# Filler products on TensorE, first loads in another order, and the third batch's attention moved: one-core linear attention with two MoE layers

## The chip, the cores and the metric

The kernel runs on one core of a Trainium2 chip. A core has five engines that run side by side, each through its own instructions in order: PE (TensorE, matrix products; PEld is its weight load), DVE (VectorE), ACT (ScalarE), POOL (GpSimd) and SP (SyncE, which here only issues DMAs). They wait for each other through semaphores. The metric is the device time of one execution in microseconds (us), lower is better.

## The reference, cut to what matters

```python
kv  = einsum('bhsd,bhse->bhde', k, v)            # 8 batches, 8 heads, 576 tokens, 64 wide
out = einsum('bhsd,bhde->bhse', q, kv)
x   = out / sqrt(mean(out*out, -1) + 1e-6) * g_norm     # as 4608 tokens x 512
h = x @ w_in;   x = relu(h)**2 @ w_out           # layer 1: 512 -> 2048 -> 512
h = x @ w_in2;  out = (h * cos(h)) @ w_out2      # layer 2
```

q, k, v and g_norm are float32, the four weight matrices float64.

## The kernel before, in words

**Numbers.** A float64 weight is turned into two float32r halves, high and low (`words`, `value`, the end of `conv_steps`: lines L111 to L125 and L205/L206, on DVE and ACT). Activations are split likewise, so that a product is three PE products: high by high, high by low, low by high. The attention of the first two batches is done in plain float32 (L288, L314), which PE runs as several passes; later batches split the squares too (L292, L316, L317).

**Stages.** First come attention and the first two 512-token tiles of layer 1, then more attention between the tiles of layer 1, and last a recursive block scheme for the rest of both layers, which the change doesn't touch. In layer 1 a *chunk* is one 128-wide slice of the 2048 hidden units for one tile, 8 chunks to a tile. Chunk n has an in part (12 products, L379, into a PSUM bank `l` or `acc`), then relu and square on ACT (L388, L390), the split into `gh` (ACT, L393) and `gl` (DVE, L394), and, two chunks later, an out part (12 products, L416, into `acc`).

**Attention.** For one batch, 5 pieces of k and v (`kvld`) are loaded and multiplied into a 128x128 block per head pair (`kv_mm`, L258), which ACT copies to `kvx` (L271). Then 8 units follow, (p, half) with p = 0..3 a pair of heads: the product with q (`att_a`, L288), square and scaled copy on ACT (`sq` L299, `og` L300), the sum over a head by a product with a matrix of ones (`att_b`, `ss`, L314), the inverse root on ACT (`r` L319, its square L321), three DVE steps (`att_c`, L329 to L331, the last writes `xo`), the split into `xh` (ACT, L348) and `xl` (DVE, L349), and a DMA of `xo` to memory by POOL (`att_e`, L355). There are three `xo` buffers, so the fourth unit writes a buffer that the first one's DMA has to have left.

**What sets the order.** A table of times, in units of chunks, holds all jobs beside the chunks (`at(n, fn, ...)`): `starts` gives for each batch the time of its first unit and the step to the next, a weight's conversion stands at `w_at`, the load of a tile of x at `load_x`. The tile framework then makes of this an order for every engine, with its own list of what is ready. It doesn't change at run time.

**Loads.** SP issues nearly all loads, in order. It keeps eight DMAs in flight: each issue waits for the landing of the one eight before it, and for its buffer. At the start these are g_norm (`gcol`, two small ones), the float64 slices of the weights (`raw`, L151, 512 KB each), k and v (`kvld`, L246, 512 KB, the fifth 256 KB), and q (L275, 288 KB), which has 3 buffers (`NQ`) for 4 values of p.

Of the kernel before, what the change touches and what calls it, by code (L numbers as in the profile page):

```python
# [8 lines left out]
F32 = mybir.dt.float32  # L9
F32R = mybir.dt.float32r  # L10
# [6 lines left out]
P = 128  # L17
# [5 lines left out]
def kernel(  # L23
# [15 lines left out]
    nc = tc.nc  # L39
    NT, DM = out.shape  # L40
    NKC = DM // P
# [4 lines left out]
    NQ = 3  # L46
    NRAW = 4
    KVB = 5
    XB = 9
    S = NT // B  # L50
    HS = S // 2
    D = 64
    TOK = 512
# [14 lines left out]
    ones = cpool.tile([P, P], F32R, name="ones")  # L68
    gcol = cpool.tile([P, 1], F32, name="gcol")
# [18 lines left out]
    def bank_tile(tag):  # L88
        return pools["ps"].tile([P, 512], F32, tag=tag, name=tag)

    def bank(use):
        tag = banks[use].pop(0)
        banks[use].append(tag)
        return bank_tile(tag)

    def as32(ap):
        return ap.bitcast(F32)
# [144 lines left out]
    def load_kv(b, c):  # L242
# [3 lines left out]
        nc.sync.dma_start(out=t[:n], in_=kv[r0:r0 + n])  # L246
        kv_sb[b, c] = t

    def kv_mm(b, c):
        n = min(P, S - c * P)  # L250
        if c == 0:
            kv_ps[b] = bank("o").rearrange("p (c d) -> p c d", d=P)
        t = kv_sb.pop((b, c))
        for p in range(NKC):
            for j in range(2):
                r = slice(j * D, (j + 1) * D)
                head = slice(p * P + j * D, p * P + (j + 1) * D)
                nc.tensor.matmul(  # L258
                    kv_ps[b][r, p, r],
                    t[:n, 0, head],  # L260
                    t[:n, 1, head],
                    start=(c == 0 and p == 0),
                    stop=(c == NSC - 1),
                    skip_group_check=True,
                )
        if c == NSC - 1:
            ps = kv_ps.pop(b)
            kvs[b] = kvx[b % 2]
            for j in range(2):
                r = slice(j * D, (j + 1) * D)  # L270
                nc.scalar.copy(out=kvs[b][r, :, r], in_=ps[r, :, r])  # L271

    def load_q(b, p):
        t = att_p.tile([P, S], F32, tag="q", name="q", bufs=NQ)
        nc.sync.dma_start(out=t, in_=qT[p * P:(p + 1) * P, b * S:(b + 1) * S])  # L275
        q_sb[b, p] = t

# [32 lines left out]
    def att_b(*u):  # L310
        og, sh, sl = att[u]
        ss = bank("ss")[:, :HS]
        if u[0] < NEXACT:
            nc.tensor.matmul(ss, as32(ones[:]), sh[:], start=True, stop=True)  # L314
        else:
            nc.tensor.matmul(ss, ones[:], sh[:], start=True, stop=False)  # L316
            nc.tensor.matmul(ss, ones[:], sl[:], start=False, stop=True)  # L317
        r = att_p.tile([P, HS], F32, tag="r", name="r", bufs=2)
        nc.scalar.activation(out=r, in_=ss, func=AF.Abs_reciprocal_sqrt, scale=1.0 / D, bias=epsb)  # L319
        r2 = att_p.tile([P, HS], F32, tag="r2", name="r2", bufs=2)  # L320
        nc.scalar.activation(out=r2, in_=r, func=AF.Square)  # L321
        att[u] = (og, ss, r, r2)
# [39 lines left out]
    def att_units(b):  # L362
        return [(b, p, i) for p in range(NKC) for i in range(2)]
# [43 lines left out]
    def layer_out(t, f):  # L407
        wh, wl = (x[:, 1, :] for x in wts[0, f])
        gh, gl = gs.pop((t, f))
        for i in range(NKC):  # L410
            if f == 0:
                accs[i] = bank_tile(f"acc{i}")
            o = accs[i]
            cs = slice(i * P, (i + 1) * P)
            for n, (a, m) in enumerate(((wh, gh), (wh, gl), (wl, gh))):
                nc.tensor.matmul(  # L416
                    o, a[:, cs], m[:], start=(f == 0 and n == 0), stop=(f == NH - 1 and n == 2), skip_group_check=True
                )
            if f == NH - 1:
                evict(t, i, o)  # L420
# [254 lines left out]
    def at(n, fn, *a):  # L675
        jobs.append((n, len(jobs), fn, a))
# [48 lines left out]
    w_stream = Stream(load_w, conv_w, w_items)  # L725
    w_stream.place(w_at, 0.5, range(2 * NH - NRAW, 2 * NH - NRAW + 2))
    late_stream = Stream(load_w, conv_w, [("pairs", 1, p, 0) for p in range(1, 2 * NP)])
    late_stream.place([pos(n) for n in (0.95, 2.5, 3.25, 4.5, 6.4, 8.7, 10.75)], 0, lead=0.5)

    kv_stream = Stream(load_kv, kv_mm, [(b, c) for b in range(B) for c in range(NSC)])  # L730
    starts = [(-13, 1), (-3, 0.8)] + [(-3 + 7 * (b - 1), 7 / (2 * NKC)) for b in range(2, B)]
    kv_stream.place([s0 - 0.5 for s0, _ in starts for c in range(NSC)], 0)
    q_items = [(b, p) for b in range(B) for p in range(NKC)]
    for b, (s0, ds) in enumerate(starts):
        for i, u in enumerate(att_units(b)):
            n = s0 + i * ds
            if u[2] == 0:
                at(n, att_a, *u)
                if len(q_items) > NQ:
                    at(n, load_q, *q_items[NQ])  # L740
                q_items = q_items[1:]
            for fn in (att_b, att_c, att_d):
                at(n + 1.5, fn, *u)
            at(n + 2.5, att_e, *u)
    for t in range(NDIRECT, NTILE):
        n0 = t * NH
        for q in range(2):
            at(n0 - (6.2, 3 if t == 2 else 4.2 if t == 3 else 5.1)[q], load_x, t, q)
        for c in range(NKC):
            at(n0 - 3.2 + 0.8 * c, split_x, t, c)  # L750

# [37 lines left out]
    def run_jobs(n):  # L789
        nonlocal done  # L790
        while done < len(jobs) and jobs[done][0] <= n:
            _, _, fn, a = jobs[done]
            done += 1
            fn(*a)

    def run_chunks(lo, hi):
        for n in range(lo, hi):
            if n < LAG:
                if n == 0:
                    first = layer_in(0, *range(LAG))  # L800
                    banks["l"] = ["l0"]
                ps = first[n]
            else:
                ps, = layer_in(*chunks[n])
            gs[chunks[n]] = act_relu2(ps, n < nAtt)
            run_jobs(n)
            if n >= LAG:
                layer_out(*chunks[n - LAG])
            run_jobs(n + 0.5)
# [42 lines left out]
        run_jobs(here)  # L852

    for j in range(2):
        nc.sync.dma_start(out=gcol[j * D:(j + 1) * D, :], in_=g_norm.rearrange("(d o) -> d o", o=1))
    nc.vector.memset(epsb, EPS)
    nc.scalar.activation(out=zerob, in_=epsb, func=AF.Abs_reciprocal_sqrt)
    nc.vector.memset(zerob, 0.0)
# [6 lines left out]
    with ExitStack() as early:  # L865
        pools["ps"] = early.enter_context(tc.tile_pool(name="ps0", bufs=1, space=PSUM))
        def right(name, bufs):
            return early.enter_context(tc.tile_pool(name=name, bufs=bufs, side="right"))

        right("pad", 1).tile([P, 56], F32, name="pad")  # L870
        ev_p, pools["raw"] = right("ev", 2), right("conv", 2)
        x_p, g_p, pools["t"] = (right(n, b) for n, b in (("x", XB), ("g", 3), ("tmp", 8)))
        with tc.tile_pool(name="att", bufs=1, side="right") as att_p:
            kvx = [att_p.tile([P, NKC, P], F32, tag=f"kvx{b}", name=f"kvx{b}") for b in range(2)]
            for x in kvx:
                nc.gpsimd.memset(x, 0.0)
            w_stream.advance(2)
            kv_stream.advance(KVB)
            w_stream.advance(NRAW - 2)
            for p in range(NQ):  # L880
                load_q(0, p)
            run_jobs(-1)
            banks.update(o=["o", "l1"], ss=["ss"], l=["l0", "acc3"])
            run_chunks(0, nAtt)
        pools["x"] = ctx.enter_context(tc.tile_pool(name="xb", bufs=13, side="left"))
        banks["l"] = ["l0", "l1", "o", "ss"]
        run_chunks(nAtt, nA0)
        for c in chunks[-LAG:]:
            layer_out(*c)
# [48 lines left out]
```

## Time and profile before

| | us |
|---|---|
| median of 3 runs (1570.99 to 1572.47) | 1571.52 |
| the profiled execution | 1568.49 |
| its span, first to last instruction | 1566.6 |
| PE busy | 1535.3 (98%) |
| DVE busy | 1294.4 (83%) |
| ACT busy | 1073.3 (69%) |

The profile is one execution. Its own time is 1568.49 us, 1.9 us more than its span and 3.0 us less than the median of the runs. Matmuls overlap in the pipeline, so a row of PE is longer than the step from one product to the next.

### The profile page before, as it was taken

The numbers are of one execution on the slowest core, as the hardware profiler recorded it, in microseconds if no ns is written. First come the engines' busy times: TensorE is split into PE (matmuls) and PEld (weight loads), VectorE is DVE, ScalarE is ACT, GpSimd is POOL, SyncE is SP. The second block draws the span as 40 slices with busy tenths as digits, with TensorE's granted clock in tenths as the row PEclk, the third lists the DMA queues.
The fourth block names the chain that finished last, engine by engine and source line by source line (L and its number), as shares of the span: only waits on it lengthen the run. The fifth ranks groups of instructions, "written<-read, shape, count | busy, mean of one in ns | idle before, by whom it ended". The sixth has DMA issues, their size and how long they took to land.

```text
span 1566.6 us, 24649 instructions
## 1 busy us (share of the span) xinstructions
PE 1535.3 (98%) x9104; PEld 1346.2 (86%) x9104; DVE 1294.4 (83%) x1744; ACT 1073.3 (69%) x1528; POOL 107.7 (7%) x171
## 2 busy tenths in 40 slices
PE   5999999999999999999999999999999999999998
PEld 4777777778887888888998899999999999999998
DVE  7987888888875899989889879867986788679777
ACT  5977777785443766656556777777777777777774
POOL 1112111110000000000000000000000000001000
PEclk9999999999999999999999999999999999999999
DMA  9858888867578979898998978887888789999895
GB/s 320 284 156 238 279 276 248 246 210 221 179 238 282 328 239 382 300 379 274 380 327 333 344 218 255 252 285 215 255 247 282 215 248 270 305 326 289 294 315 149
DMA packets 222151, 426.31 MB, mean 272 GB/s; under 512 B 18000, under 2 KB 138064, under 8 KB 222032
## 3 DMA queue, kind: packets, MB, share of 16 engines
q1 hardware_dynamic: 210560, 390.13, 73.0%
q0 software_dynamic: 11472, 34.61, 10.4%
q8 instruction: 73, 1.20, 0.3%
q14 instruction: 46, 0.38, 0.1%
HBM read 317.72 MB, written 81.79 MB: 255 GB/s over the span
## 4 chain that ended last, share of the span: by engine, by line
PE 81%; DVE 8%; DMA 4%; ACT 4%; issue 3%; SPq 0%; POOL 0%; DVEq 0%; ACTq 0%; POOLq 0%
PE SB L629 15%; PE FA L505 15%; PE FB L505 15%; PE SA L629 15%; PE acc L416 9%; PE l L379 7%; PE o L379 1%; DMA ws_d<-raw 1%; PE ss L379 1%; DMA xraw<-x_d 1%; DMA q<-in_qT 1%; DVE gl L606 1%; DMA sum<-part 1%; DVE sum L657 1%; DMA raw<-in_wA 1%
## 5 line engine op out<-in xcount | busy, mean ns | idle before, releaser
L505 PE MATMUL FA<-xh,wi 128*128 128x512 f32 (+1 forms) x840 | 301.4, 370 | 2.3 <-ACT FA L537 1.5
L505 PE MATMUL FB<-xh,wi 128*128 128x512 f32 (+1 forms) x840 | 301.3, 370 | 0.3 <-DVE h L530 0.3
L629 PE MATMUL SB<-ws,gh 128*128 128x256 f32 x1008 | 233.1, 280 | 0.5 <-ACT part L654 0.5
L629 PE MATMUL SA<-ws,gh 128*128 128x256 f32 x1008 | 232.8, 280 | 0.4 <-ACT y L564 0.4
L629 PEld LDWEIGHTS SA<-ws,gh 128*128 128x128 f32 x1008 | 183.5, 188 | 12.6 <-ACT y L564 0.5
L629 PEld LDWEIGHTS SB<-ws,gh 128*128 128x128 f32 x1008 | 183.3, 188 | 12.5 <-ACT part L654 0.7
L505 PEld LDWEIGHTS FA<-xh,wi 128*128 128x128 f32 x840 | 157.1, 188 | 12.2 <-ACT FA L537 1.9
L505 PEld LDWEIGHTS FB<-xh,wi 128*128 128x128 f32 x840 | 157.3, 188 | 10.3 <-DVE h L530 0.6
L629 PE MATMUL SB<-ws,gl 128*128 128x256 f32 x504 | 141.4, 280 | 1.1 <-DVE gl L606 1.1
L606 DVE TENSOR_TENSOR gl<-y,gh 128x1024 fp32r<-128x1024 f32 (+1 forms) x100 | 111.4, 1114 | 36.8 <-ACT gh L605 36.6
L629 PE MATMUL SA<-ws,gl 128*128 128x256 f32 x504 | 141.3, 280 | 0.5 <-DVE gl L606 0.5
L572 DVE SCALAR_TENSOR_TENSOR y<-y,h 128x1024 f32<-128x1024 f32 (+1 forms) x80 | 89.1, 1114 | 48.4 <-ACT y L568 48.4
L655 POOL DMA_DIRECT2D sum<-part x53 | 45.6, 860 | 1138.0 <-ACT part L654 541.4
L554 ACT ACTIVATE y<-h,zerob 128x1024 int32<-128x1024 f32 (+1 forms) x80 | 85.0, 1063 | 52.0 <-DVE h L530 52.0
L416 PE MATMUL acc<-gh,wh 128*128 128x512 f32 x288 | 113.6, 395 | 0.0
L416 PE MATMUL acc<-gl,wh 128*128 128x512 f32 x288 | 112.9, 392 | 0.0
L416 PE MATMUL acc<-gh,wl 128*128 128x512 f32 x288 | 112.6, 391 | 0.0
L505 PE MATMUL FA<-xl,wi 128*128 128x512 f32 (+1 forms) x300 | 110.9, 370 | 0.0
L505 PE MATMUL FB<-xl,wi 128*128 128x512 f32 (+1 forms) x300 | 110.9, 370 | 0.0
L629 PEld LDWEIGHTS SB<-ws,gl 128*128 128x128 f32 x504 | 94.9, 188 | 7.4 <-DVE gl L606 1.5
L629 PE MATMUL SA<-gh,ws 128*128 128x512 f32 (+1 forms) x280 | 100.7, 369 | 0.3 <-issue 0.3
L564 ACT ACTIVATE y<-y 128x1024 f32<-128x1024 f32 (+1 forms) x80 | 78.0, 975 | 33.5 <-DVE y L558 33.4
(171 smaller groups left out, 3816.7 us busy)
## 6 DMA issues: line engine op xcount, KB each, us to landing
wi<-wi_d SPq DMA_DIRECT2D x210, 512.0 KB, 6.7
ws<-ws_d SPq DMA_DIRECT2D x210, 512.0 KB, 5.4
sum<-part POOLq DMA_DIRECT2D x33, 512.0 KB, 7.5
kvld<-in_kv SPq DMA_DIRECT2D x32, 512.0 KB, 6.5
ws_d<-raw SPq DMA_DIRECT2D x24, 448.0 KB, 4.2
q<-in_qT SPq DMA_DIRECT2D x32, 288.0 KB, 5.0
p_d<-ev SPq DMA_DIRECT2D x18, 512.0 KB, 4.1
raw<-in_wA SPq DMA_DIRECT2D x16, 512.0 KB, 7.2
```

The lines of the kernel that those rows point to most:

```text
L379: nc.tensor.matmul(ps, a[:, 0, cs], m[:], start=(c == 0 and k == 0), stop=(c == NKC - 1 and k == 2))
L416: nc.tensor.matmul(o, a[:, cs], m[:], start=(f == 0 and n == 0), stop=(f == NH - 1 and n == 2), skip_group_check=True)
L505: nc.tensor.matmul(ps[:, pp, :], a, b, start=(n == 0 and (i in (0, 2) or i == 1 and not seeded(k))), stop=(n == 5), skip_group_check=True,)
L554: nc.scalar.activation(out=y.bitcast(I32), in_=hs[k, b], func=AF.Identity, bias=zerob)
L564: nc.scalar.activation(out=y, in_=y, func=AF.Sin, scale=math.pi)
L572: nc.vector.scalar_tensor_tensor(out=y, in0=y, scalar=-2.0 * math.pi, in1=hs.pop((k, b)), op0=ALU.add, op1=ALU.mult)
L606: nc.vector.tensor_tensor(out=l, in0=src, in1=as32(h), op=ALU.subtract)
L629: nc.tensor.matmul(ps[:, b, :], lhs, rhs, start=(n == 0 and (m == 0 or b % 2 == 0) and i in (0, 1, 2)), stop=(n == 5), skip_group_check=True,)
L655: nc.gpsimd.dma_start(out=e, in_=part, accum_op=ALU.add)
L657: nc.vector.tensor_tensor(out=e, in0=ps, in1=e, op=ALU.add)
```

## The change

PE gets products whose result is never read: 26 of a zeroed tile with the matrix of ones before the first product of k and v, 2 behind the first batch's last one, and one beside each `ss` product of the first batch (8). All write the PSUM bank `l1`, which is free then. The loads of `gcol` go from SP to ACT's DMA queue. All four q of the first batch are loaded before the fourth `raw` (before: three, behind the fourth `raw`, and the last one far later), the q of p = 3 of the first two batches into the buffers `ev`, which are free until the first tile ends. The third batch's attention starts at 5.5 chunks and takes 0.65 chunks a unit (before: 4 and 0.875), and the third tile's first x is loaded 0.6 chunks later.

```diff
+    def warm(lhs, rhs, times=1):
+        for _ in range(times):
+            nc.tensor.matmul(idle[:, :rhs.shape[-1]], lhs, rhs, start=True, stop=True, skip_group_check=True)
...
         if c == NSC - 1:
+            if b == 0:
+                warm(as32(ones[:n]), t[:n, 0, :448], 2)
...
-        t = att_p.tile([P, S], F32, tag="q", name="q", bufs=NQ)
+        if b < 2 and p == NKC - 1:
+            t = ev_p.tile([P, 2, 512], F32, tag="ev", name="q").rearrange("p a n -> p (a n)")[:, :S]
+        else:
+            t = att_p.tile([P, S], F32, tag="q", name="q", bufs=NQ)
...
             nc.tensor.matmul(ss, as32(ones[:]), sh[:], start=True, stop=True)
+            if u[0] == 0:
+                warm(as32(ones[:]), sh[:])
...
-    starts = [(-13, 1), (-3, 0.8)] + [(-3 + 7 * (b - 1), 7 / (2 * NKC)) for b in range(2, B)]
+    starts = [(-13, 1), (-3, 0.8), (5.5, 0.65)] + [(-3 + 7 * (b - 1), 7 / (2 * NKC)) for b in range(3, B)]
...
-                if len(q_items) > NQ:
-                    at(n, load_q, *q_items[NQ])
-                q_items = q_items[1:]
+                if q_next < len(q_items) and (b, i) != (1, 0):
+                    at(n, load_q, *q_items[q_next])
+                    q_next += 1
...
-            at(n0 - (6.2, 3 if t == 2 else 4.2 if t == 3 else 5.1)[q], load_x, t, q)
+            at(n0 - (5.6 if t == 2 else 6.2, 3 if t == 2 else 4.2 if t == 3 else 5.1)[q], load_x, t, q)
...
-        nc.sync.dma_start(out=gcol[j * D:(j + 1) * D, :], in_=g_norm.rearrange("(d o) -> d o", o=1))
+        nc.scalar.dma_start(out=gcol[j * D:(j + 1) * D, :], in_=g_norm.rearrange("(d o) -> d o", o=1))
...
+            idle = bank_tile("l1")
+            blank = g_p.tile([P, TOK], F32R, tag="gh", name="blank")
+            nc.vector.memset(as32(blank[:]), 0.0)
+            warm(ones[:], blank[:], 26)
             w_stream.advance(2)
             kv_stream.advance(KVB)
-            w_stream.advance(NRAW - 2)
-            for p in range(NQ):
+            w_stream.advance(1)
+            for p in range(NKC):
                 load_q(0, p)
+            w_stream.advance(NRAW - 3)
```

On SP, at the very start, the kernel before stands so:

```order
L855 DMA gcol<-in_g_norm 64x1 x2
L151 DMA raw<-in_wA 128x1024 x2
L246 DMA kvld<-in_kv 128x1024 x4
L246 DMA kvld<-in_kv 64x1024
L151 DMA raw<-in_wA 128x1024 x2
L275 DMA q<-in_qT 128x576 x3
L151 DMA raw<-in_wA 128x1024
L246 DMA kvld<-in_kv 128x1024 x4
L246 DMA kvld<-in_kv 64x1024
L151 DMA raw<-in_wA 128x1024 x3
L275 DMA q<-in_qT 128x576 x3
```

and the changed one so:

```order
L151 DMA raw<-in_wA 128x1024 x2
L246 DMA kvld<-in_kv 128x1024 x4
L246 DMA kvld<-in_kv 64x1024
L151 DMA raw<-in_wA 128x1024
L284 DMA q<-in_qT 128x576 x4
L151 DMA raw<-in_wA 128x1024 x2
L246 DMA kvld<-in_kv 128x1024 x4
L246 DMA kvld<-in_kv 64x1024
L151 DMA raw<-in_wA 128x1024 x3
L284 DMA q<-in_qT 128x576 x4
```

The two small loads are gone from SP, the four q stand before the fourth `raw`, and the second batch's q come four together.

On ACT, in the first batch's first units, before (from the copy of `kvx` on):

```order
L271 COPY kvx_137<-o 64x4x64 x2
L112 ACTIVATE e<-e,expb 128x512 x2
L205 CAST wh<-w 128x512
L299 ACTIVATE sq<-acc_270 128x288
L300 ACTIVATE og<-acc_270,gcol 128x288
L299 ACTIVATE sq<-acc_271 128x288
L300 ACTIVATE og<-acc_271,gcol 128x288
L319 ACTIVATE r<-ss,epsb 128x288
```

and after:

```order
L277 COPY kvx_137<-o 64x4x64 x2
L112 ACTIVATE e<-e,expb 128x512
L308 ACTIVATE sq<-acc_303 128x288
L309 ACTIVATE og<-acc_303,gcol 128x288
L308 ACTIVATE sq<-acc_304 128x288
L309 ACTIVATE og<-acc_304,gcol 128x288
L205 CAST wh<-w 128x512
L330 ACTIVATE r<-ss,epsb 128x288
```

The cast `wh` of the third converted slice has moved behind the first unit's two squares and two copies, and the fourth slice's step `e` stands further on.

On PE, the third batch's first unit (`64x288`), before, between the in part of chunk 3 (`l_824`) and that of chunk 4 (`l_937`):

```order
L379 MATMUL l_824<-xl,wh 128x512
L379 MATMUL l_824<-xh,wl 128x512
L292 MATMUL l_970<-q,kvx_137 64x288
L292 MATMUL o<-q,kvx_137 64x288
L292 MATMUL l_970<-q,kvx_137 64x288
L292 MATMUL o<-q,kvx_137 64x288
L416 MATMUL acc_793<-gh,wh 128x512
```

and after, where `l_982` is chunk 5:

```order
L390 MATMUL l_982<-xh,wl 128x512
L427 MATMUL acc_836<-gl,wh 128x512
L427 MATMUL acc_836<-gh,wl 128x512
L427 MATMUL acc_840<-gh,wh 128x512
L427 MATMUL acc_840<-gl,wh 128x512
L427 MATMUL acc_840<-gh,wl 128x512
L427 MATMUL acc_844<-gh,wh 128x512
L427 MATMUL acc_844<-gl,wh 128x512
L427 MATMUL acc_844<-gh,wl 128x512
L301 MATMUL l_1079<-q,kvx_137 64x288
L301 MATMUL o<-q,kvx_137 64x288
```

It now comes behind the in part of chunk 5 and the rest of an out part, two chunks further on.

## Rows read from the trace of the kernel before

**Rows 1.** Waits of PE, whole span: us in total, times, longest us.
```profile
PE o L258 <- DMA kvld<-in_kv: 11.1, 4, 9.3
PE ss L316 <- DVE m L329: 2.4, 4, 0.9
PE ss L314 <- ACT sq L299: 1.9, 1, 1.9
PE acc L288 <- DMA q<-in_qT: 1.8, 1, 1.8
```
**Rows 2.** Busy by stretch: us, PE, PEld, DVE, ACT, POOL, PEclk, DMA share, GB/s.
```profile
16.59:55.60 39.01, 32.88 (x189) 23.45 (x188) 36.24 (x84) 34.27 (x87) 5.60 (x10) 1.00 0.93 331
...
62.30:139.00 76.70, 76.70 (x436) 59.04 (x440) 65.33 (x145) 59.83 (x134) 13.50 (x24) 1.00 0.66 207
139.00:400.00 261.00, 257.03 (x1494) 201.60 (x1495) 218.48 (x490) 189.36 (x410) 40.57 (x77) 1.00 0.80 243
```
**Rows 3.** PE in order of time: start, us, what [idle before <-releaser].
```profile
9.31 1.12 PE L258 MATMUL o<-kvld 128*64 128x64 f32 x16 [9.31 <-DMA kvld<-in_kv]
...
15.68 1.12 PE L258 MATMUL o<-kvld 64*64 64x64 f32 x16 [0.45 <-DMA kvld<-in_kv]
18.62 2.26 PE L288 MATMUL acc<-q,kvx 128*128 128x288 f32 x4 [1.82 <-DMA q<-in_qT]
...
24.46 0.65 PE L288 MATMUL acc<-q,kvx 128*128 128x288 f32 x2
...
35.11 1.13 PE L288 MATMUL acc<-q,kvx 128*128 128x288 f32 x4
38.16 0.75 PE L314 MATMUL ss<-sq,ones 128*128 128x288 f32 x2 [1.92 <-ACT sq L299]
...
45.14 0.61 PE L379 MATMUL acc<-xh,wh 128*128 128x512 f32 x1
...
48.12 0.39 PE L379 MATMUL l<-xh,wh 128*128 128x512 f32 x1
...
56.28 0.40 PE L416 MATMUL acc<-gl,wh 128*128 128x512 f32 x1
...
62.29 0.50 PE L379 MATMUL l<-xh,wh 128*128 128x512 f32 x1 [0.22 <-ACT r L388]
```
**Rows 4.** DVE in order of time.
```profile
6.83 0.43 DVE L111 TENSOR_SCALAR e<-raw 128x512 uint32<-128x512 uint32 x1 [2.87 <-DMA raw<-in_wA]
...
16.59 0.43 DVE L111 TENSOR_SCALAR e<-raw 128x512 uint32<-128x512 uint32 x1 [2.48 <-DMA raw<-in_wA]
...
24.00 0.46 DVE L329 SCALAR_TENSOR_TENSOR m<-ss,r 128x288 f32<-128x288 f32 x1 [0.74 <-ACT r L321]
...
25.82 0.45 DVE L331 TENSOR_TENSOR xo<-m,og 128x288 f32<-128x288 f32 x1
26.19 0.68 DVE L116 SCALAR_TENSOR_TENSOR w<-raw,w 128x512 uint32<-128x512 uint32 x1
26.79 0.45 DVE L329 SCALAR_TENSOR_TENSOR m<-acc,r 128x288 f32<-128x288 f32 x1
...
40.24 0.46 DVE L329 SCALAR_TENSOR_TENSOR m<-ss,r 128x288 f32<-128x288 f32 x1 [0.76 <-ACT r L321]
...
46.62 0.46 DVE L349 TENSOR_TENSOR xl<-xo,xh 128x288 fp32r<-128x288 f32 x1 [0.49 <-ACT xh L348]
...
54.92 0.68 DVE L394 TENSOR_TENSOR gl<-g,gh 128x512 fp32r<-128x512 f32 x1
```
**Rows 5.** ACT in order of time.
```profile
20.75 0.41 ACT L299 ACTIVATE sq<-acc 128x288 f32<-128x288 f32 x1
21.06 0.49 ACT L300 ACTIVATE og<-acc,gcol 128x288 f32<-128x288 f32 x1
21.44 0.41 ACT L299 ACTIVATE sq<-acc 128x288 f32<-128x288 f32 x1
...
59.83 0.62 ACT L205 CAST wh<-w 128x512 fp32r<-128x512 f32 x1 [1.76 <-DVE w L125]
...
61.64 0.59 ACT L388 ACTIVATE r<-l 128x512 f32<-128x512 f32 x1
```
**Rows 6.** SP's issues in order of time; one q of 22.65 (to landing); a piece of the chain.
```profile
0.74 1.23 SPq L855 DMA_DIRECT2D gcol<-in_g_norm  x2
2.02 1.05 SPq L151 DMA_DIRECT2D raw<-in_wA  x2
...
22.65 3.79 SPq L275 DMA_DIRECT2D q<-in_qT  x3
...
q<-in_qT SPq DMA_DIRECT2D x1, 288.0 KB, 10.3
...
8.06 10.42 DMA q<-in_qT
```
**Rows 7.** DMAs of `xo`: the first; landings at 20 to 50; at 82 to 106.
```profile
26.59 0.71 POOL L355 DMA_DIRECT2D x_d<-xo  x1 [24.87 <-DVE xo L331]
...
DMA to landing us min/median/max: 3.0/5.5/7.0
...
x_d<-xo POOLq DMA_DIRECT2D x9, 144.0 KB, 5.3
...
x_d<-xo POOLq DMA_DIRECT2D x8, 72.0 KB, 2.0
```
**Rows 8.** The third tile's last `xl` (L233 on DVE, 139 to 148), and PE's use of it.
```profile
L233 DVE TENSOR_TENSOR xl<-xraw,xh x2: 682/687/692, 139.4 to 143.0; 128x512 fp32r<-128x512 f32 x2
...
147.68 0.39 PE L379 MATMUL l<-xl,wh 128*128 128x512 f32 x1
```

More of the change, by code (lines that the diff above doesn't have):

```diff
@@ L730 @@
     kv_stream = Stream(load_kv, kv_mm, [(b, c) for b in range(B) for c in range(NSC)])
-    starts = [(-13, 1), (-3, 0.8)] + [(-3 + 7 * (b - 1), 7 / (2 * NKC)) for b in range(2, B)]
+    starts = [(-13, 1), (-3, 0.8), (5.5, 0.65)] + [(-3 + 7 * (b - 1), 7 / (2 * NKC)) for b in range(3, B)]
     kv_stream.place([s0 - 0.5 for s0, _ in starts for c in range(NSC)], 0)
     q_items = [(b, p) for b in range(B) for p in range(NKC)]
+    q_next = NKC
     for b, (s0, ds) in enumerate(starts):
```

## The prediction

> **What bounds the kernel now.** Read the waits of PE first [rows 1]. The reader is to see that PE waits little, and early: 11.1 us for the first k and v, 1.8 for the first q, 1.9 for the first squares. Then the stretches [rows 2]: from 62.30 to 139 PE is busy for all 76.70 us, and from 139 to 400 it lacks 261.00 - 257.03 = 4.0. So the work of PE behind 62.3 is a solid block, and the kernel ends earlier only by what that block starts earlier, apart from those 4.0 us.
>
> Next: what lets the block start? PE in order of time [rows 3] seems to say that it is dense from chunk 1 at 45.14 on. But its products need things from DVE. DVE in the stretch from 16.59 to 55.60 is busy for 36.24 of 39.01 us [rows 2], and its low half `gl` of chunk 1, which starts at 54.92 and ends at 55.60 [rows 4], is used by PE at 56.28 [rows 3]: 0.7 us of slack. Then chunk 3 at 62.29 waits for ACT to drain its bank [rows 3]; that drain, at 61.64, stands in ACT's order behind a cast that waited 1.76 us for DVE [rows 5]. PE is full, but it follows DVE by less than a microsecond. That is the bound at the place where the change works.
>
> **The change part by part.** The order of DVE up to the `gl` of chunk 1 holds the same instructions before and after, but for one memset: from the third weight slice's first step (16.59) on 84 of them, the 36.24 us above. So this `gl` can end earlier by just two things, an earlier start and fewer waits in between. The waits before are 39.01 - 36.24 = 2.77 us.
>
> *The start.* SP spends 0.74 to 2.02 on the two small loads, and the first `raw` follows at 2.02 [rows 6]. Without them every load up to the third `raw` is issued 1.28 us earlier. These loads land one behind the other without a gap, so the third lands 1.28 earlier too, and DVE starts at 15.31 for 16.59 [rows 4]: -1.28. It can't be less than 0 or more than 1.28. The small loads on ACT cost ACT's queue about 1.2 us when it has nothing else to do before 5.5.
>
> *The fillers and the four q.* The clock first: the granted clock reads 1.00 in every stretch, but the same four records of L288 take 2.26 us at 18.62 and 1.13 at 35.11 [rows 3], a ratio of 2.0, so the first ran at the lower level of 1.2 GHz, the other at 2.4. PE had worked in pieces from 9.31 on and was still slow; at 24.46, in products back to back since 18.62, it is fast (0.65 for two records). The 26 fillers are as wide as chunk 1's products, 12 of which take 48.12 - 45.14 = 2.98 us, 0.25 each [rows 3]: 6.5 us at the full rate, 12.9 at half. They start near 2.0 (the zeroed tile) and end between 8.5 and 14.9; the k and v pieces land 1.28 earlier than [rows 3], the first at 8.0, the last at 14.4. I take it that the rate rises among them, as it did in the unbroken products from 18.62 on, and that they end before 11: then the pieces wait for nothing but their loads. The last piece's products then end at 15.0 (before 15.68 + 1.12 = 16.8). The two fillers behind it take two products of 448 columns, 448/288 x 0.5 = 0.8 each, until 16.5; the copies of `kvx` end at 15.9, so these fillers cost 0.5. The first q, behind 1.28 us of small loads and one `raw` less, lands at 18.48 [8.06 + 10.42, rows 6] less about 2.5 = 16.0. So attention starts at 16.5 and not at 18.62, and its first squares are there at 17.1 and not at 20.75 [rows 5]. Eight more fillers of 0.5 beside the `ss` products lie in time that PE spends waiting for ACT.
>
> What do these 3.6 us give DVE? Two waits go: 0.74 at 24.00, where DVE waited for the root of a slow `ss` product, and 0.76 at 40.24, behind the fourth q, which was issued at 22.65 or later and landed ten microseconds on. The 0.49 at 46.62 [rows 4] goes as well, as ACT is less behind there. Together -1.99.
>
> What comes new? First, the cast `wh` of the third slice now stands on ACT behind two `sq` and two `og`. They run from 17.1 for 2 x (0.31 + 0.38) = 1.4 [rows 5], so the cast ends at 19.0 with its 0.5. DVE's next step needs it and was ready at 18.0: +1.1. Then the first unit's `m` needs a root that comes 0.45 later: +1.55 in all, between 0 (the cast done first) and 2.5 (the squares later by the fillers). Second, the three `xo` buffers. A DVE step takes 0.37 at 288 columns (25.82 to 26.19) and 0.60 at 512 (26.19 to 26.79) [rows 4]. In the new order the first `xo` is begun at 21.7, the second 4 steps of 512 and 5 of 288 later at 26.0, the third and the fourth 4 steps each, at 27.6 and 29.1. A buffer is free when its DMA has landed: 0.45 for `xo` itself, 0.3 to POOL's issue (25.82 to 26.59), 5.3 to landing [rows 4, 7], 6.0 together. So the fifth unit can't write before 32.0 and the sixth not before 33.6, where DVE would be there at 30.6 and 33.1: +1.4 and +0.4. Before, the units were too slow to meet this. With the fastest landing, 3.0, it would be nothing, with the slowest, 7.0, 3.5 [rows 7]; I take 1.8, the middle, since the median was taken under the same load, a DMA share of 0.93 [rows 2].
>
> A rule on that: a write of `xo` takes 5.3 us among the loads and 2.0 without [rows 7]. The Trainium skill, DMA: Bandwidth & Descriptors (Queues, rings and completion order), says that each DMA engine goes round between the queues that have work, packet by packet, so a write from POOL should get its turn beside SP's loads and not stand behind all of them. By the rule the +1.8 would shrink or go, by the row it stays. The row decides for the forecast; the rule belongs to the first rival.
>
> Sum for DVE at the `gl` of chunk 1: -1.28 - 1.99 + 1.55 + 1.8 = +0.1 us. PE arrives at chunk 1 some 5 us earlier than 45.14, and gives that back in front of this `gl` and of the bank of chunk 3.
>
> *The third batch.* Its first unit moves two chunks down. PE is full from 62.3 to 139, so nothing can be won there. It takes load off DVE and ACT around chunks 4 and 5, where they are closest to full, and puts it where DVE has room (65.33 of 76.70 over the whole stretch [rows 2]): 0, with -1 to +3 for the waits behind 139. The later load of x: 0, with the same cover.
>
> Total 1568.49 + 0.1 = 1568.6 in the profiled execution, and 3.0 more for the median: 1571.6, no change.
>
> **The rivals.**
> *Faster: the new waits don't come.* If the writes land in 2 to 3 us or the cast goes first, DVE loses less. With both gone the sum is -3.3: 1568.2. The floor is an earlier start and no wait at all, -1.28 - 2.77 = -4.05: 1567.5. For it: a landing of 3.0 us occurs [rows 7], and PE and ACT have slack. Against: 5.3 us and the order on ACT.
>
> *Slower: the fillers stay slow.* At half rate they end at 14.9, five pieces of 1.12 [rows 3] follow until 20.5, two fillers of 1.6 until 23.7: attention starts 7.2 us later than I say. DVE's first `m` stands before the fourth conversion, so DVE waits as long, less the 1.8 of buffers: +5.5, 1577. It decides once the two fillers end later than 18.6, where the first q product stood before. For it: PE was still slow after its pieces from 9.31 to 16.8. Against: products back to back had brought the rate by 24.46, and a pause of 1.92 before 38.16 didn't cost it [rows 3]. The Trainium skill, TensorE: Matmul & The Clock Gate (Part 1: The HAM clock gate), has the throttle as the default state, lifted by activity and put back in idleness; fillers that end too early would then be lost, since PE idles again before the last piece. The 1.92 us speaks against that here.
>
> *Slower: the third tile's x comes late.* The last `xl` is done at 143.0 + 0.7 and used at 147.68 [rows 8]: 4.0 us of slack. The third batch, now closer together, feeds it. If ACT or DVE fall behind by more than 4.0 us, every further microsecond is PE's; 7 us late gives +3, 1574.6.
>
> **How the numbers follow.** Forecast 0.62, faster rival 0.24, slow fillers 0.07, late x 0.07. A measurement of this kernel tells about 0.2%, 3.1 us, from no change. The forecast's own spread, +-2 us for the bounds of the two new waits, lies within that but for 0.02 on either side. Of the faster rival 0.19 is beyond 3.1 us and 0.05 within. Slow fillers are all beyond, late x 0.05 beyond and 0.02 within. So faster 0.21, same 0.65, slower 0.14. The range goes from the floor, less 0.5 for the spread of a median, 1567.0, to the late x, 1574.5.
>
> **What would show it.** The first `raw` step of DVE at 5.5 and the third at 15.3 (start). L297 in 1.1 us for four records at 16.5 (fillers). Chunk 1 on PE near 40, and then a wait of PE for DVE's `gl` or for ACT's drain of a bank before chunk 3, several microseconds in all, where there is 0.2 now. DVE waiting for a DMA of `xo` near 31. Chunk 3 at 62 +- 2. I am wrong if chunk 3 starts before 60, if PE has its 5 us still at 62, or if PE's waits behind 139 grow over 4.0 us.

## The result, and the profile after

| | before | after |
|---|---|---|
| median, us (6 runs each) | 1572.2 | 1582.82 |
| the profiled execution | 1568.49 | 1581.94 |
| its span | 1566.6 | 1580.2 |

The changed kernel takes 1.0070 of the time before, 95% interval 1.0060 to 1.0081: 10.6 us slower, where no change was forecast. It is outside the range, on the side to which 0.14 was given.

The stretches first, with the columns of [rows 2]:

```profile
16.59:55.60 39.01, 34.19 (x180) 24.34 (x179) 30.09 (x71) 28.80 (x74) 5.06 (x9) 0.83 0.81 298
62.30:139.00 76.70, 75.61 (x484) 57.13 (x483) 64.64 (x142) 59.11 (x132) 11.31 (x22) 1.00 0.62 198
139.00:400.00 261.00, 253.56 (x1471) 197.51 (x1470) 214.45 (x484) 190.75 (x415) 43.62 (x80) 0.99 0.80 242
```

In the first stretch DVE is busy for 30.09 us where it was busy for 36.24: the engine that set the pace now stands idle. PE, in order of time:

```profile
13.48 0.69 PE L262 MATMUL o<-kvld 128*64 128x64 f32 x16 [1.71 <-DMA kvld<-in_kv]
15.02 0.68 PE L262 MATMUL o<-kvld 64*64 64x64 f32 x16 [0.86 <-DMA kvld<-in_kv]
15.63 2.86 PE L251 MATMUL l<-kvld,ones 64*128 64x448 f32 x4
18.42 2.29 PE L297 MATMUL acc<-q,kvx 128*128 128x288 f32 x4
...
39.33 1.13 PE L297 MATMUL acc<-q,kvx 128*128 128x288 f32 x4
44.27 1.33 PE L323 MATMUL acc<-sq,ones 128*128 128x288 f32 x2 [3.81 <-ACT sq L308]
...
50.68 0.61 PE L390 MATMUL acc<-xh,wh 128*128 128x512 f32 x1
...
68.73 0.50 PE L390 MATMUL l<-xh,wh 128*128 128x512 f32 x1 [1.09 <-ACT r L399]
```

Against [rows 3]: the first q products start at 18.42 for 18.62 and are as slow as before; the two wide fillers take 2.86 us in front of them. Chunk 1 starts at 50.68 for 45.14, chunk 3 at 68.73 for 62.29. The granted clock, in stretches cut where it changes (busy time of PE, PEld, DVE, ACT, POOL, then PEclk):

```profile
1.88:16.20 14.32, 11.75 (x108) 9.21 (x109) 6.88 (x15) 4.44 (x8) 0.00 (x0) 1.00 0.94 318
16.20:23.00 6.80, 6.80 (x14) 3.73 (x13) 3.21 (x6) 3.58 (x8) 0.00 (x0) 0.50 1.04 417
23.00:43.50 20.50, 16.44 (x133) 12.06 (x131) 16.27 (x43) 15.82 (x43) 3.98 (x7) 1.00 0.98 356
43.50:50.30 6.80, 6.03 (x13) 4.47 (x14) 6.24 (x14) 6.16 (x17) 0.77 (x2) 0.50 0.61 197
```

The 26 fillers brought 2.4 GHz, but PE paused for 1.71 and 0.86 us between the pieces of k and v, and from 16.20, where the wide fillers and the first q products stand, it had 1.2 GHz again. It had 1.2 GHz once more from 43.50; PE waits 3.81 us up to 44.27. (Ahead of the first change of the clock that a profile holds, the column reads 1.00 whatever the clock was: of the 26, the slowest took 0.80 us and the median one 0.40. The first stretch of [rows 2] reads 1.00 likewise, over the slow products of 18.62.) DVE, with what ended its idle time:

```profile
7.57 0.15 DVE L875 TENSOR_SCALAR gcol<-gcol 128x1 f32<-128x1 f32 x1 [3.99 <-DMA gcol<-in_g_norm]
...
15.97 0.43 DVE L111 TENSOR_SCALAR e<-raw 128x512 uint32<-128x512 uint32 x1 [1.06 <-DMA raw<-in_wA]
...
22.09 0.69 DVE L206 TENSOR_TENSOR wl<-w,wh 128x512 fp32r<-128x512 f32 x1 [3.30 <-ACT wh L205]
24.17 0.46 DVE L340 SCALAR_TENSOR_TENSOR m<-ss,r 128x288 f32<-128x288 f32 x1 [1.39 <-ACT r L332]
...
35.85 0.46 DVE L342 TENSOR_TENSOR xo<-m,og 128x288 f32<-128x288 f32 x1 [1.06 <-DMA x_d<-xo]
37.21 0.46 DVE L342 TENSOR_TENSOR xo<-m,og 128x288 f32<-128x288 f32 x1 [0.19 <-DMA x_d<-xo]
...
42.76 0.46 DVE L342 TENSOR_TENSOR xo<-m,og 128x288 f32<-128x288 f32 x1 [1.75 <-DMA x_d<-xo]
...
60.57 0.69 DVE L405 TENSOR_TENSOR gl<-g,gh 128x512 fp32r<-128x512 f32 x1
```

Chunk 1's `gl` ends at 61.25, 5.65 us later than the 55.60 of [rows 4]. From 15.97 to there DVE is idle for 9.4 us, where it was idle for 2.8 before from its third slice on. Most of this is three waits: at 22.09 DVE waits 3.30 us for the cast `wh`, which stands on ACT behind the first squares, at 24.17 it waits 1.39 us for the first root, and from 35.85 on 3.0 us in all for buffers of `xo`. The last passes through ACT, whose cast of that `xo` holds up the squares behind it, and these hold PE at 44.27:

```profile
15.81 0.74 ACT L277 COPY kvx<-o 64x256 f32<-64x256 f32 x2 [1.62 <-PE o L262]
...
19.79 0.41 ACT L308 ACTIVATE sq<-acc 128x288 f32<-128x288 f32 x1 [2.49 <-PE acc L297]
...
43.26 0.52 ACT L359 CAST xh<-xo 128x224 fp32r<-128x224 f32 x2 [2.85 <-DVE xo L342]
```

The DMAs of the first 60 us (KB each, median us from issue to landing):

```profile
x_d<-xo POOLq DMA_DIRECT2D x10, 144.0 KB, 5.0
...
gcol<-in_g_norm ACTq DMA_DIRECT2D x2, 0.2 KB, 5.7
```

The last loss has no idle time at all. PE in the third batch, some q products in order of time, in the kernel before and then in the changed one:

```profile
88.41 0.45 PE L292 MATMUL l<-q,kvx 64*64 64x288 f32 x1
...
89.05 0.50 PE L416 MATMUL acc<-gh,wh 128*128 128x512 f32 x1
```

```profile
88.20 0.69 PE L301 MATMUL l<-q,kvx 64*64 64x288 f32 x2
88.83 0.50 PE L390 MATMUL l<-xh,wl 128*128 128x512 f32 x1
...
91.34 0.45 PE L301 MATMUL o<-q,kvx 64*64 64x288 f32 x1
91.35 0.45 PE L301 MATMUL l<-q,kvx 64*64 64x288 f32 x1
91.36 0.68 PE L301 MATMUL o<-q,kvx 64*64 64x288 f32 x2
...
98.40 0.70 PE L301 MATMUL l<-q,kvx 64*64 64x288 f32 x2
```

One q, which serves a pair of units, has four products of 64 rows by 64 columns (eight records), on the four quarters of the array, into two banks `l` and `o`. In the kernel before these eight stand together, and from the first of them to the next other product it is 0.64 us (88.41 to 89.05). Here two into `l` stand alone at 88.20, the other six at 91.34; and the two alone take 0.63 us to the next product as well.

### The profile page after: what moved, and what is told of

Read it like the earlier page. It is cut to its first block, busy times and chain, and to the rows that moved or that the text cites. A ratio compares the mean times of both kernels' runs of the same rounds, so it can differ in the third digit from the quotient of the medians.

```text
span 1580.2 us, 24743 instructions
## 1 busy us (share of the span) xinstructions
PE 1552.7 (98%) x9150; PEld 1358.0 (86%) x9150; DVE 1294.3 (82%) x1745; ACT 1075.3 (68%) x1528; POOL 107.7 (7%) x171
## 4 chain that ended last, share of the span: by engine, by line
PE 82%; DVE 7%; DMA 6%; ACT 2%; issue 1%; SPq 0%; DVEq 0%; ACTq 0%
PE SB L640 16%; PE FA L516 16%; PE SA L640 16%; PE FB L516 16%; PE acc L427 8%; PE l L390 6%; DMA ws_d<-raw 2%; DMA x_d<-xo 1%; PE o L390 1%; DMA xraw<-x_d 1%; DMA raw<-in_wB 1%; PE ss L390 1%; DMA kvld<-in_kv 1%; DVE m L340 0%; DVE raw L194 0%
## 5 line engine op out<-in xcount | busy, mean ns | idle before, releaser
L640 PE MATMUL SB<-gh,ws 128*128 128x512 f32 (+1 forms) x280 | 100.6, 369 | 0.4 <-issue 0.4
```

The source lines that it names most:

```text
L640: nc.tensor.matmul(ps[:, b, :], lhs, rhs, start=(n == 0 and (m == 0 or b % 2 == 0) and i in (0, 1, 2)), stop=(n == 5), skip_group_check=True,)
```

## The experiments

The theories named below: A, the new first loads delay DVE or ACT; A', the three `xo` buffers bind in the new order; B, the fillers stand in the way; C, the third batch's move costs by itself; D, what is lost further down is an echo of an earlier delay. The first four kernels are the changed one with a part undone.

**No fillers.**
```diff
-            warm(ones[:], blank[:], 26)
-                warm(as32(ones[:n]), t[:n, 0, :448], 2)
-                warm(as32(ones[:]), sh[:])
```


> The changed kernel without any filler product and without the zeroed tile; loads and third batch as changed. Theory A (the loss of the first 62 us, some 6 us, comes from the loads: g_norm on ACT's queue lands late and holds DVE and the fifth k and v; the fillers neither help nor harm much): 1581 to 1584, like the changed kernel's 1582.8. Rival B (the fillers themselves delay the first q products, which ran at half rate behind them): 1576 to 1579.

**Third batch as before.**
```diff
-    starts = [(-13, 1), (-3, 0.8), (5.5, 0.65)] + [... for b in range(3, B)]
+    starts = [(-13, 1), (-3, 0.8)] + [... for b in range(2, B)]
```
Here and in each kernel below that moves the third batch, the third tile's first x moves with it, by the 0.6 chunks of the change.

> The changed kernel with the third batch's attention and the third tile's first x load where they were before. Theory C (the third batch, closer together, costs about 2 us of PE between chunks 6 and 13 and is behind the 5.6 us lost in tiles 3 to 5): about 7 us back, 1575 to 1577. Rival D (what is lost behind chunk 3 is an echo of the later start): 1580 to 1583.

**g_norm on SP again.**
```diff
-        nc.scalar.dma_start(out=gcol[j * D:(j + 1) * D, :], ...)
+        nc.sync.dma_start(out=gcol[j * D:(j + 1) * D, :], ...)
```


> The changed kernel with the two small g_norm loads back at the head of SP's queue, all else as changed. Theory A: DVE's first weight step at 6.8 (7.64 in the changed kernel), the fifth k and v no longer late, 1 to 3 us back: 1580 to 1582. Rival (g_norm's place means nothing, DVE would have waited elsewhere): 1582.8 as changed.

**All first loads as before** (the last edit, the q of p = 3 and the later ones back in their old buffers and places, and):
```diff
-            for p in range(NKC):
-                load_q(0, p)
-            w_stream.advance(NRAW - 3)
+            w_stream.advance(NRAW - 3)
+            for p in range(NQ):
+                load_q(0, p)
```


> The changed kernel with all first loads in the old order (g_norm on SP, three q behind the fourth weight slice, three q buffers); fillers and third batch as changed. Theory A: chunk 3 on PE back near 62 to 64 (68.7 in the changed kernel), 1576 to 1579. Rival B (fillers): still above 1581.

Then each part alone on the kernel before, its lines as in the change.

**Only the fillers.**
```diff
+            warm(ones[:], blank[:], 26)
+                warm(as32(ones[:n]), t[:n, 0, :448], 2)
+                warm(as32(ones[:]), sh[:])
```


> The kernel before with the fillers alone (36 products and the zeroed tile). Theory A (fillers harmless, little use): 1570 to 1574, the first squares some 1 to 2 us earlier than 20.75. Rival B (fillers delay the attention): 1576 or more.

**Only the third batch.**
```diff
+    starts = [(-13, 1), (-3, 0.8), (5.5, 0.65)] + [... for b in range(3, B)]
```


> The kernel before with the third batch's move alone (and the 0.6 chunks of the third tile's x). Theory C: 5 to 8 us slower, 1577 to 1580, with PE waiting for DVE's m of later batches. Rival D (echo of the late start): 1571 to 1574.

**Only the loads** (with the q of p = 3 in the buffers `ev`, as in the change).
```diff
...
+            w_stream.advance(1)
+            for p in range(NKC):
+                load_q(0, p)
...
+        nc.scalar.dma_start(out=gcol[j * D:(j + 1) * D, :], ...)
```


> The kernel before with the new first loads alone (g_norm on ACT, four q early, the fourth q in the ev buffers). Theory A: 3 to 6 us slower, 1575 to 1578, chunk 3 at 65 to 69. Rival (loads alone are a gain and only meet the fillers badly): 1568 to 1571.

**The changed kernel with a fourth buffer.**
```diff
-        xo = att_p.tile([P, HS], F32, tag="xo", name="xo", bufs=3)
+        xo = att_p.tile([P, HS], F32, tag="xo", name="xo", bufs=4)
```


> The changed kernel with four xo buffers for three. Theory A': the waits of DVE for a DMA of xo (1.1, 0.2 and 1.8 us at 35 to 43) go, PE's 3.8 us wait at 44.3 shrinks below 2 and the clock isn't lost at 43.5 to 50.3; 3 to 5 us back: 1578 to 1580. Rival (the waits are taken by the next thing in DVE's order): 1581 to 1583.

**The kernel before, unchanged, a second profile.** (No edit.)

> The kernel before, unchanged, for a second profile. The first profile of it took 1568.49 us, 3.0 less than the median of its runs. Every other kernel profiled so far gains 2.5 to 5.6 us on it between chunk 27 and chunk 40, where nothing was changed. If that is how this stretch differs from one execution to the next (theory R), the second profile shows such a loss too and takes 1570 to 1575 us. If it is an echo of the change, further down (theory D), the second profile agrees with the first within 1 us there and ends at 1568 to 1569.

**The kernel before with a fourth buffer** (the edit of two kernels above).

> The kernel before with four xo buffers for three, nothing else. In the trace of before DVE waits for no write of xo. Theory A' (the buffers bind only where the units come closer together, as in the new order): no change, 1571.5 +- 1.5, ratio 0.999 to 1.001. Rival (three buffers hold the order that the scheduler makes as well, and so cost the kernel before too): 1567 to 1569.5.

**Early q with a fourth buffer:** only the loads, g_norm on SP, `bufs=4`.
```diff
+            for p in range(NKC):
+                load_q(0, p)
-        xo = att_p.tile([P, HS], F32, tag="xo", name="xo", bufs=3)
+        xo = att_p.tile([P, HS], F32, tag="xo", name="xo", bufs=4)
```


> Before, with the four q of the first batch loaded early (and the second batch's together), g_norm on SP as before, and four xo buffers; no fillers, third batch as before. Theory A with A': the new q loads alone cost 2.7 us, of which the late g_norm is one part and the three buffers the other; with both put right the earlier fourth q is worth what DVE waited for it, 0.8 to 1.5 us: 1569.5 to 1571, DVE waits for xo under 0.5 us up to 60. Rival (the loss is that 1.2 us of q stand ahead of the fourth raw and of the second batch's k and v, and so those come late): 1573 to 1575, and DVE waits for raw or ACT instead.

**The same with fillers that hold the clock.**
```diff
+            warm(ones[:], blank[:], 26)
+        if b == 0:
+            warm(ones[:], blank[:], (2, 2, 6, 4, 3)[c])
```


> As the kernel with early q and four xo buffers sent beside it, plus fillers that are to hold the clock: the 26 at the start, and 2, 2, 6, 4 and 3 more of 512 columns behind the first batch's five pieces of k and v, so that PE has no pause until the last piece has landed near 15.6; none behind the squares and none of 448 columns. Theory B (fillers fail because PE pauses for 0.5 to 1.6 us between the pieces and the clock falls at 16): the granted clock stays full from 6 on, four records of the first q products take 1.1 us for 2.3, first squares at 17.5 to 18.5 for 20.7, and 1.0 to 2.0 us less than its neighbour. Rival (DVE sets the pace whatever PE does): the clock is full and the time is the same within 0.7 us.

**The third batch less late, and in other groups:** two kernels, each the edit of "Only the third batch" with other numbers.
```diff
-    starts = [(-13, 1), (-3, 0.8), (5.5, 0.65)] + ...
+    starts = [(-13, 1), (-3, 0.8), (4.5, 0.8)] + ...
```


> Before with the third batch at 4.5 chunks and 0.8 a unit (before: 4 and 0.875, the change: 5.5 and 0.65); the third tile's first x 0.6 chunk later as in the change. In PE's order the four q products of a unit stand together for three of the third batch's units and are split 2 and 2 for one: 5 groups for 4. Theory S (a group of q products of two records holds PE as long as one of eight, 0.63 us for 0.65, so every extra group costs 0.63): chunk 11 later by 0.6 than with whole groups, and the time 1572 to 1573. Rival (the later third batch costs by its waits on ACT and DVE, whatever the grouping): the loss by chunk 11 is over 1.2 us.


```diff
-    starts = [(-13, 1), (-3, 0.8), (5.5, 0.65)] + ...
+    starts = [(-13, 1), (-3, 0.8), (5, 0.7)] + ...
```


> Before with the third batch at 5 chunks and 0.7 a unit; x as beside it. The q products stand in 8 groups for 4 units. Theory S: 4 extra groups, 2.5 us by the end of the third batch, more than the change's own 3 extra groups (1.9), though the batch lies half a chunk nearer to where it was: 1574 to 1575. Rival (lateness costs, not the grouping): less than the change's third batch alone, under 1.5 us by then, 1572 to 1573.5.

**Only the 26 fillers; only the other ten.**
```diff
+            warm(ones[:], blank[:], 26)
```


> Before with the 26 fillers at the start alone. Theory B1 (the first 26 end before the first k and v and only the ten later ones cost, since they stand in front of products that ACT and DVE wait for): 1571.5 +- 1, chunk 3 within 0.7 of before. Rival (the clock, raised and lost again, costs by itself): the loss of all fillers together, 1575 to 1577, with the clock at half from 16 to 23.


```diff
+                warm(as32(ones[:n]), t[:n, 0, :448], 2)
+                warm(as32(ones[:]), sh[:])
```


> Before with the ten later fillers alone: two of 448 columns behind the first batch's last k and v, and one beside each of its eight sums of squares. Theory B1: all of the fillers' loss, 1575 to 1577, first q products 1.2 us later or more (the two of 448 run at half rate until about 20), chunk 3 later by 2 to 3.5. Rival (26 fillers' clock): under 1 us.

What was measured. The ratio is to the kernel before, timed on the same chip. The other columns tell how much later than in the second profile of the kernel before a chunk's first product starts, in us; each is one profiled execution. Those of "loads as before" and of the ten fillers are the fastest of their kernels' 10 and 12 runs, 4 us under the median.

| kernel | median | ratio, 95% interval | chunk 1 | 3 | 11 | 48 |
|---|---|---|---|---|---|---|
| changed | 1582.82 | 1.0070, 1.0060 to 1.0081 | 5.3 | 6.2 | 8.4 | 11.2 |
| no fillers | 1578.13 | 1.0042, 1.0027 to 1.0057 | 3.3 | 4.2 | 6.3 | 5.6 |
| third batch as before | 1578.6 | 1.0046, 1.0031 to 1.0061 | 5.4 | 6.2 | 6.2 | 8.7 |
| g_norm on SP | 1581.21 | 1.0061, 1.0044 to 1.0078 | 6.1 | 7.0 | 9.1 | 8.8 |
| loads as before | 1577.03 | 1.0036, 1.0024 to 1.0048 | -0.6 | 1.1 | 3.3 | 2.2 |
| fourth buffer | 1576.85 | 1.0033, 1.0022 to 1.0043 | 0.5 | 1.6 | 3.7 | 7.4 |
| only fillers | 1576.56 | 1.0029, 1.0018 to 1.0040 | 2.2 | 2.9 | 3.0 | 4.0 |
| only third batch | 1574.88 | 1.0017, 1.0008 to 1.0026 | 0.1 | 0.0 | 2.2 | 2.7 |
| only loads | 1574.58 | 1.0011, 0.9999 to 1.0022 | 2.0 | 2.9 | 2.8 | 3.1 |
| before, first profile | 1572.2 | | -0.2 | -0.2 | -0.2 | -2.9 |
| before, fourth buffer | 1572.5 | 0.9996, 0.9987 to 1.0005 | 1.4 | 1.4 | 1.4 | 2.1 |
| early q, fourth buffer | 1571.98 | 0.9990, 0.9979 to 1.0002 | 0.9 | 2.0 | 1.9 | 1.9 |
| the same, clock held | 1575.58 | 1.0010, 1.0000 to 1.0021 | 1.4 | 2.4 | 2.4 | 4.0 |
| third batch 4.5, 0.8 | 1572.25 | 1.0000, 0.9990 to 1.0009 | 1.5 | 1.5 | 1.7 | 1.5 |
| third batch 5, 0.7 | 1575.53 | 1.0019, 1.0008 to 1.0030 | 0.4 | 0.4 | 3.2 | 4.9 |
| only 26 fillers | 1572.37 | 1.0000, 0.9992 to 1.0009 | -0.1 | -0.1 | 0.0 | 1.0 |
| only ten fillers | 1574.6 | 1.0014, 1.0002 to 1.0025 | 1.5 | 3.1 | 3.2 | 0.3 |

Some expectations were missed: the third batch alone (1577 to 1580) and the ten fillers (1575 to 1577) cost less than expected, the third batch put back (1575 to 1577) and early q with a fourth buffer (1569.5 to 1571) gave less, the fourth buffer in the changed kernel gave more (1578 to 1580), and the held clock gave none of its 1.0 to 2.0 us.

*How far one profile can be read.* The second profile of the kernel before took 1570.95 us and lost 3.3 us against the first between chunks 28 and 38, with nothing changed (theory R of its expectation). Where the kernel before lacked 261.00 - 257.03 = 4.0 us of PE in [rows 2], it now lacks 5.5:

```profile
38.70:42.10 3.40, 3.40 (x9) 2.38 (x8) 2.47 (x7) 3.27 (x10) 0.54 (x1) 0.50 0.97 336
62.30:139.00 76.70, 76.50 (x432) 58.99 (x432) 65.47 (x146) 60.44 (x135) 13.32 (x24) 1.00 0.66 208
139.00:400.00 261.00, 255.45 (x1484) 200.69 (x1483) 215.94 (x484) 188.67 (x408) 40.95 (x77) 0.99 0.79 242
```

So theory D falls, and of the 13.5 us between the two first profiles some 3 are chance. At chunk 1 too two kernels without a change of time stand 1.4 and 1.5 later; only more than that says something there. The clock at half from 38.70 had no visible price, since chunk 1 came 0.2 us later than in the first profile. Further down, where PE is full, it had one. Two rows of PE in the second profile, the stretch between them, and the same two products in the first profile:

```profile
287.51 0.51 PE L379 MATMUL l<-xh,wh 128*128 128x512 f32 x1 [1.67 <-ACT r L388]
...
291.23 0.42 PE L379 MATMUL l<-xh,wh 128*128 128x512 f32 x1
```

```profile
287.88:291.29 3.41, 3.41 (x10) 2.64 (x9) 3.38 (x8) 3.35 (x9) 0.00 (x0) 0.50 0.72 203
```

```profile
285.62 0.50 PE L379 MATMUL l<-xh,wh 128*128 128x512 f32 x1 [1.40 <-ACT r L388]
...
287.80 0.39 PE L379 MATMUL l<-xh,wh 128*128 128x512 f32 x1
```

Behind a wait that was 0.3 us longer the clock fell, and nine products took 3.72 us for 2.18: 1.5 of the 3.3 us. Five profiles show no half clock from 230 to 300: the first of the kernel before, no fillers, g_norm on SP, loads as before, and the ten fillers. From chunk 11 to 48 these five move by -2.9 to -0.3 us in the table, the others by -0.2 to 3.7. That the clock makes the whole of this difference isn't shown.

*The three parts.* Alone they cost 4.65, 2.97 and 2.67 us by their medians, 10.3 together for the whole of 10.6 (by the ratios 9.0 for 11.0). Taken out of the changed kernel one at a time, they give back 3.8 (fillers), 3.3 (third batch) and 4.9 us (loads). Each has an interval of some 3 us or more, so that the parts add up is not shown to the microsecond; the loads seem dearer beside the others than alone.

*The `xo` buffers (A').* A fourth one takes the changed kernel from 10.6 to 4.9 us, and chunk 1 from 5.3 to 0.5. Its waits of DVE from 14 to 70 (us, times, longest), and the PE row that stands for the one at 44.27:

```profile
DVE wl L206 <- ACT wh L205: 4.7, 3, 3.8
...
DVE xo L342 <- DMA x_d<-xo: 0.2, 1, 0.2
```

```profile
41.78 0.75 PE L323 MATMUL acc<-sq,ones 128*128 128x288 f32 x2 [2.22 <-ACT sq L308]
```

The wait for `xo` is all but gone, PE is there 2.5 us earlier, and the clock holds in its trace through 43 to 50. The kernel before, where DVE waits for no `xo`, gains nothing from a fourth buffer. The new loads aren't the only thing that makes three bind: with the ten fillers alone DVE waits 1.4 us for them. With the loads alone DVE waits 2.0 us for them, and with the fourth buffer (and g_norm on SP) the ratio goes from 1.0011 (0.9999 to 1.0022) to 0.9990 (0.9979 to 1.0002): no loss, and no gain that can be told from none. g_norm on SP alone gave back at most 1.6 us of medians whose intervals overlap, and chunk 1 came no earlier.

*The fillers (B).* The 26 alone cost nothing, though the clock fell back in their run too. Two of its stretches:

```profile
4.61:15.60 10.99, 7.84 (x85) 6.05 (x83) 6.53 (x12) 2.57 (x4) 0.00 (x0) 1.00 1.01 343
15.60:22.40 6.80, 4.78 (x24) 3.57 (x25) 5.24 (x11) 4.18 (x9) 0.00 (x0) 0.50 1.04 416
```

The other ten alone give 1.0014 (1.0002 to 1.0025), 2.1 us by the medians. So 26 and ten apart leave 2.6 of the 4.65 us that all fillers cost together without an account, though the intervals overlap (1.0018 to 1.0040 for all). PE with these ten, and then DVE's first `m` and its `gl` of chunk 1:

```profile
16.91 3.35 PE L251 MATMUL l<-kvld,ones 64*128 64x448 f32 x4
20.19 2.29 PE L297 MATMUL acc<-q,kvx 128*128 128x288 f32 x4
```

```profile
25.60 0.46 DVE L340 SCALAR_TENSOR_TENSOR m<-ss,r 128x288 f32<-128x288 f32 x1 [2.15 <-ACT r L332]
...
58.28 0.68 DVE L405 TENSOR_TENSOR gl<-g,gh 128x512 fp32r<-128x512 f32 x1
```

The wide two run until 20.2, 1.6 us behind the first q products of [rows 3]; DVE waits 2.15 us for its first root where it waited 0.74 [rows 4], later it waits 1.4 us for an `xo` buffer, and chunk 1's `gl` ends at 58.96 for 55.60.

Was the idea sound and only badly done? The kernel that fills PE's pauses answers a part of that. PE in it, and the stretch in which the clock held:

```profile
17.82 0.68 PE L262 MATMUL o<-kvld 64*64 64x64 f32 x16
...
19.46 1.21 PE L297 MATMUL acc<-q,kvx 128*128 128x288 f32 x4 [0.52 <-issue]
```

```profile
8.00:28.00 20.00, 17.42 (x134) 12.01 (x133) 13.37 (x27) 11.09 (x27) 0.72 (x1) 1.00 1.04 359
```

The four q records take 1.21 us for 2.29, as theory B wanted. But the fillers stand in PE's order, the last piece of k and v is multiplied at 17.82 where its neighbour without fillers has it at 16.08, and the first squares come at 20.22, not before 18.5, where the neighbour's come at 19.48. Behind 28 the clock wasn't held: it read 0.50 from 28.40 to 35.20, as the neighbour's did from 27.80 to 34.60. The kernel is no faster than its neighbour. How much a held clock would give without this delay wasn't tried; a hint is that in the second profile of the kernel before the products are fast from 22.0 on, in [rows 3] from 24.5, and chunk 1 came 0.2 us later in spite of it.

*The third batch (C).* Busy time of its q products alone (the first two columns after the length are PE and PEld), in the kernel before (its second profile, 4 groups of records), with 4.5 and 0.8 (5 groups), moved alone (7), and with 5 and 0.7 (8):

```profile
62.00:112.00 50.00, 3.00 (x32) 0.97 (x32) 1.00 0.59 190
```

```profile
70.00:109.00 39.00, 3.55 (x32) 1.01 (x32) 1.00 0.51 162
```

```profile
72.00:112.00 40.00, 4.93 (x32) 1.37 (x32) 1.00 0.44 138
```

```profile
70.00:110.00 40.00, 5.62 (x32) 1.55 (x32) 1.00 0.46 141
```

The same 32 records, 0.55 to 0.7 us for each further group. The delay between chunks 3 and 11 follows it: 0.2 for one group more (0.6 expected), 2.2 for three, 2.8 for four. All six kernels with the change's third batch lose 2.1 to 2.2 us there, those with the old one -0.1 to 0.1. The rival, that lateness costs, falls: the batch at 5 is less late than the change's at 5.5 and costs more by chunk 11 (the medians, 3.1 and 3.0 us, don't tell them apart). The records of a group overlap (91.34, 91.35 and 91.36 above), and each group, of two records or of eight, holds PE for some 0.65 us. Why the order splits them (the bank of one comes free earlier than that of the other, and each product is placed by itself) is read from the code and wasn't tried.

None of these kernels beats the one before.

## Why the prediction was wrong

*What bounds.* Right: PE follows DVE up to chunk 3, and what is lost there stays lost.

*The start, -1.28.* The third slice came at 15.97, -0.62. The two small loads took 5.7 us from ACT's queue, so that DVE's first step on `raw` came at 7.64, where 5.5 was forecast and 6.83 was before. Giving them back to SP brought nothing measurable, so this term decided little.

*The fillers and the four q.* The first failed step. It put the first q products at 16.5 "in 1.1 us", because the clock would rise among the fillers and stay, as it had over a pause of 1.92 us [rows 3]. It rose and didn't stay: 0.50 from 16.20. The Trainium skill, TensorE: Matmul & The Clock Gate (Part 1: The HAM clock gate), has the throttle as the default state, lifted by activity and put back in idleness. The prediction set that aside for the one row; the trace after, where the clock went back behind pauses of 1.71 and 0.86 us, agrees with it. The wide fillers took 2.8 us for the 1.6 forecast and held the q products until 18.42, 1.9 us behind the copies of `kvx` (done at 16.55) for 0.5; with these products at half rate the squares came at 19.79 for 17.1. So the term that hangs on them grew: the cast `wh` and the first `m` cost DVE 3.30 + 1.39 = 4.7 us for 1.55, and the wait of 0.74 for the first root, which should have gone, is part of that 1.39. Not all of this is the fillers': without them the squares come at 18.83, and DVE still waits 1.54 us for the cast.

*The `xo` buffers, +1.8.* The second failed step, and the dearest. The prediction named the right wait, which came near 36 instead of 31 and at 3.0 us; but it priced only DVE's own idle time. With what followed on ACT, PE and the clock it was worth 4.8 us at chunk 1 and 5.7 us of the median, as the fourth buffer shows. A write of `xo` took 5.0 us, close to the row's 5.3. The Trainium skill, DMA: Bandwidth & Descriptors (Queues, rings and completion order), has each DMA engine go round between the queues that have work. It gives no time for a write; that this one would be quicker was the prediction's own inference, and 5.0 us doesn't bear it out. (The row of 2.0 beside the 5.3 is of writes of half the size, 72 KB.)

*The third batch, 0.* The third failed step. "PE is full from 62.3 to 139, so nothing can be won there" is no reason that nothing can be lost: a full engine takes every longer product as it comes. The bounds of -1 to +3 held the 2.1 us, but the reason given for them (waits behind 139) was the wrong one.

*The rivals.* The faster one didn't come, since both new waits came and were longer than forecast. Slow fillers (1577) had the right part, but for another reason: the fillers were fast, and lost. Late x of the third tile didn't come: PE's waits behind 139 are for `m` (6.8 us), and the second profile of the kernel before has 3.9 of these.

*What stays open.* What the 26 and the ten fillers cost together beyond what they cost apart has no account. Of the 2.8 us that the changed kernel loses between chunks 11 and 48 against the second profile, the runs don't tell chance from cause.

## What to carry to other kernels

A filler on an in-order engine is free only where nothing behind it is awaited when it ends; price it at the slow clock. Units brought closer together need one more buffer if the DMA that empties a buffer is slower than the new step. And where an engine is full, read the new order for products that used to stand together and run side by side: their time shows as busy, in no view of waits.

## What the hardware showed unexpectedly

Two records of 64x64 products take as long as eight (0.63 against 0.64 us from the first to the next other product). Two tiny loads took 5.7 us to land from ACT's queue beside SP's 512 KB loads, and 2.3 us ahead of these from SP. The granted clock fell to half at different places in nearly every profile, as in the second one of the kernel before, where the first had it full: from 38.70 to 42.10 with no visible price, and from 287.88 to 291.29 for 1.5 us.
